# Neighbouring heads paired, w1 in one transfer, and a new opening order in a fused attention and expert kernel

## The chip, the cores and the metric

The kernel runs on one core of a Trainium2 chip. The metric is the device time of one execution in microseconds (us). Two executions of the same kernel differ by one or two per cent here, so kernels are compared by the runs of the same rounds on the same chip. Each run is marked fast or slow (slow: more than 1.5% above the fastest of its kernel), and verdicts use fast runs alone, with a 95% interval.

## The reference, cut to what matters

Two stages in one launch. First attention with short windows: 8 batches, 8 heads, 576 positions, 64 values per head. Heads 0 to 3 ("plain") see the last 32 positions, heads 4 to 7 ("dilated") every fourth of the last 128. Then a mixture of experts that picks one expert per batch.

```python
scores = (q @ k.transpose(0, 1, 3, 2)) / sqrt(64)        # [8, 8, 576, 576]
mask_plain = (rel >= 0) & (rel < 32)                     # heads 0..3
mask_dil   = (rel >= 0) & (rel < 128) & (rel % 4 == 0)   # heads 4..7
attn_out = softmax(where(mask, scores, -1e9)) @ v
x = attn_out.transpose(0, 2, 1, 3).reshape(8, 576, 512)  # head h is columns 64h..64h+63
logits = x.mean(axis=1) @ w_gate                         # [8, 8]
e = argmax(logits)                                       # one expert per batch
out = softmax(logits)[e] * (relu(x @ w1[e]) @ w2[e])     # w1: 512 x 1024, w2: 1024 x 512
```

## The kernel before: the parts that matter

A tile holds 128 partitions. Plain q and k are loaded with one transfer per batch: partition p holds 18 consecutive rows of the four heads laid end to end, so heads 0 and 1 lie in the lower 64 partitions and heads 2 and 3 in the upper 64. The loads turn float32 into bf16 on the way and are issued by GpSimd.

```python
def load_1(b, g, nm):                      # g == 0: plain heads, g == 1: dilated heads; RJ = 18
    nc.gpsimd.dma_start(
        out=loads[b][nm, g][:],
        in_=src[nm][b, 4 * g : 4 * g + 4].rearrange("h s d -> (h s) d").rearrange("(p j) d -> p j d", j=RJ))
```

TensorE turns each half of the tile with 64 x 64 transposes, so that a slot of attention works on one head of the lower half and one of the upper half at once: heads 0 and 2, then 1 and 3. Four slots make a batch, the dilated ones first. The rows of `w1` must follow the order of the heads in x, so each half of each chunk of 128 rows comes from another place and `w1` takes four transfers:

```python
for a in range(2):
    for g in range(2):
        r0 = 256 * g + 128 * a
        nc.gpsimd.dma_start(
            out=w1b[half(a), 2 * g : 2 * g + 2, f0 : f0 + fs],
            in_=moe_w1[ds(e_val, 1), r0 : r0 + 128, f0 : f0 + fs].rearrange("e (h d) f -> d (e h) f", d=DH))
load_vb(b + 2)          # GpSimd goes on issuing, in this order, for later batches
load_w2(e_val, w2b)
load_qa(b + 3); load_va(b + 3); load_qb(b + 3)
```

The expert is known only after the attention of its batch, so `w1` and `w2` cannot be loaded earlier. GpSimd issues everything in program order, loads that are needed two batches later and weights that are needed at once. In the steady part TensorE interleaves ffn1 (x times w1) and ffn2 (times w2) of batch b with the attention of batch b + 1.

The softmax here doesn't subtract the row's maximum and nothing guards it: scores larger than these inputs give would overflow.

Of the kernel before, what the change touches and what calls it, by code (L numbers as in the profile page):

```python
# [15 lines left out]
AF = mybir.ActivationFunctionType  # L16
# [3 lines left out]
P = 128  # L20
# [3 lines left out]
DH = 64  # L24
# [20 lines left out]
def kernel(  # L45
# [50 lines left out]
        return pools["M"].tile([P, 512 if dt == F32 else 1024], dt, name="m", tag="M", space=PSUM)[:]  # L96


    src = {"q": q, "k": k}
    loads = {}  # L100

# [8 lines left out]
        loads[b] = t  # L110

    def load_1(b, g, nm):
        nc.gpsimd.dma_start(
            out=loads[b][nm, g][:],
            in_=src[nm][b, 4 * g : 4 * g + 4].rearrange("h s d -> (h s) d").rearrange("(p j) d -> p j d", j=RJ),
        )

    def load_qk(b, g):
        for nm in ("k", "q"):
            load_1(b, g, nm)  # L120
# [24 lines left out]
    def load_va(b):  # L145
        if b < B:
            load_v(b, GO[0])
            load_vt(b, GO[0])
# [17 lines left out]
    dtt = const.tile([P, 4, 16], I32, name="dtt")  # L166
    for a in range(2):
        nc.gpsimd.iota(dtt[:, 2 * a : 2 * a + 2, :], pattern=[[1, 2], [2, 16]], base=32, channel_multiplier=-1)
    load_qk(0, GO[1])
    load_va(0)  # L170
    load_vb(0)
    load_qa(1)
    load_va(1)
# [7 lines left out]
    ones1 = const.tile([1, P], F32, name="ones1")  # L181
    nc.vector.memset(ones1[:], 1.0)
    wg_t = const.tile([P, 4, E], F32, name="wg_t")
    for a in range(2):
        for g in range(2):
            r0 = 256 * g + 128 * a
            nc.sync.dma_start(
                out=wg_t[64 * a : 64 * a + 64, 2 * g : 2 * g + 2, :],
                in_=moe_w_gate[r0 : r0 + 128, :].rearrange("(h d) e -> d h e", d=DH),
            )  # L190

    ident2 = const.tile([P, DH], BF16, name="ident2")
    nc.vector.tensor_tensor(out=ident2[:], in0=identb[:, 0:DH], in1=identb[:, DH:P], op=ALU.add)
# [51 lines left out]
    def emit_T(b, g, nm, banks=None):  # L245
        s = state(b)
        if g not in s["qk"]:
            s["qk"][g] = qkp.tile([P, 2, 2 * S], BF16, name="qk", tag="qk")
        qk = s["qk"][g][:, 0 if nm == "k" else 1, :]
        ld = loads[b][nm, g]  # L250
        tps = [early_bank(x, k, BF16) if banks else bank(BF16) for x, k in banks or ((0, 0), (0, 0))]
        ev = []
        if g == 0:
            for jh in range(2):
                tp = tps[jh][:, 0 : RH * DH].rearrange("p (j d) -> p j d", d=DH)
                for j in range(RH):
                    for u in range(2):
                        nc.tensor.transpose(  # L258
                            out=tp[half(u), j, :], in_=ld[half(u), RH * jh + j, :], identity=ident2[half(u), :]
                        )  # L260
                o = qk.rearrange("p (n j) -> p n j", j=RJ)[:, :, RH * jh : RH * jh + RH]
                i = tp.rearrange("p j n -> p n j")
                ev.append((o, i))
        else:
            for jh, (j0, j1) in enumerate(((0, 5), (5, 9))):
                tp = tps[jh][:, 0 : (j1 - j0) * P].rearrange("p (j n) -> p j n", n=P)
                for j in range(j0, j1):
                    nc.tensor.transpose(  # L268
                        out=tp[:, j - j0, :], in_=ld[:, 2 * j : 2 * j + 2, :].rearrange("p j d -> p (j d)"), identity=identb[:]
                    )  # L270
                o = qk.rearrange("p (n j) -> p n j", j=RH)[:, :, j0:j1]
                i = tp.rearrange("p j n -> p n j")
                ev.append((o, i))

        def on_dve():
            nc.vector.tensor_copy(out=ev[0][0], in_=ev[0][1])  # L276

        def on_act():
            nc.scalar.activation(out=ev[1][0], in_=ev[1][1], func=AF.Copy)  # L279

        return on_dve, on_act


    def emit_S_mm(b, n):
        s = state(b)
        g, h2 = GO[n // 2], n % 2
        qk = s["qk"][g]
        ps = ps0
        s["ps"] = ps

        def mm(a, e, o, lhsT, rhs):
            nc.tensor.matmul(  # L292
                ps[half(e), a, o : o + rhs.free_size()], lhsT=lhsT, rhs=rhs, start=True, stop=True, skip_group_check=True
            )

        if g == 0:
            kT = [qk[half(a), 0, S * h2 : S * h2 + S] for a in range(2)]
            qT = [qk[half(a), 1, S * h2 : S * h2 + S] for a in range(2)]
            for i in range(4):
                for e in range(2):  # L300
                    for a in range(2):
                        p0 = 128 * i + 64 * e
                        mm(a, e, QB * i, kT[a][:, p0 : p0 + KB], qT[a][:, p0 : p0 + QB])
            for a in range(2):
                mm(a, 0, 4 * QB, kT[a][:, 512:S], qT[a][:, 512:S])
            return

        u1 = (QB, 144)
        for i in range(4):
            o = HALF * (2 * (i // 2) + h2)  # L310
            for e in range(2):
                for a in range(2):
                    kc, qc = (qk[half(a), x, o : o + HALF].rearrange("p (m c) -> p c m", c=2)[:, i % 2, :] for x in range(2))
                    mm(a, e, QB * i, kc[:, 64 * e : 64 * e + KB], qc[:, 64 * e : u1[e]])
        for hh in range(2):
            o = HALF * (2 * hh + h2)
            for a in range(2):
                qc = qk[half(a), 1, o : o + HALF].rearrange("p (m c) -> p c m", c=2)
                mm(a, 0, 4 * QB + 32 * hh, qk[half(a), 0, o + 224 : o + HALF], qc[:, :, 128:144])
# [17 lines left out]
    def av_work(b, n):  # L337
# [26 lines left out]
            lasts.append(x)  # L364

        def V(a, e, i):
            return vm[half(e), 2 * a + h2, i, :]

        def pc(a, e, lo, hi):
            return pt[half(e), a, 0 : 4 * QB].rearrange("p (i n) -> p i n", n=QB)[:, :, lo:hi]  # L370
# [12 lines left out]
        def part_a():  # L383
# [8 lines left out]
                        mm(a, o + w * i, w, V(a, e, i), r, i == 0)  # L392
            if g == 0:
                for a in range(2):
                    mm(a, NLO + 256, 64, vt[:, 2 * a + h2, :], pt[half(0), a, 4 * QB : NP], False)
            for e in range(2):
                for a in range(2):
                    one = ones64[half(e), :]
# [23 lines left out]
        def part_b():  # L422
# [10 lines left out]
            if g == 0:  # L433
                for e in range(2):
                    for a in range(2):
                        o = DSO if e == 0 else DLO + 64
                        mm(
                            a, o, 256, ones64[half(e), :], pc(a, e, 64, 96), False,
                            lambda x: x.rearrange("p (i n) -> p i n", n=64)[:, :, 0:32],
                        )  # L440
            else:
                for r in range(2):
                    for a in range(2):
                        mm(
                            a, NLO, 320, vt[:, 2 * a + h2, r, :], pt[half(0), r, 4 * QB + 32 * a : 4 * QB + 32 * a + 32], False,
                            lambda x, r=r: tcls(x, 80)[:, r, :, 64:80],
                        )
                for a in range(2):
                    mm(a, DLO, 320, ones64[half(0), :], clss(a, 0, 64, 96), False, lambda x: tcls(x, 80)[:, :, :, 0:32])
                for a in range(2):  # L450
                    tl = pt[half(0), :, 4 * QB + 32 * a : 4 * QB + 32 * a + 32].rearrange("p t (c m) -> p t c m", c=2)
                    mm(a, DLO, 320, ones64[half(0), :], tl, False, lambda x: tcls(x, 80)[:, :, :, 64:80])
# [59 lines left out]
    def emit_gate(b):  # L512
# [14 lines left out]
        s["w1"], s["w2"] = w1b, w2b  # L527
        fs = F // 2 if b == 0 else F
        for f0 in range(0, F, fs):
            for a in range(2):  # L530
                for g in range(2):
                    r0 = 256 * g + 128 * a
                    nc.gpsimd.dma_start(  # L533
                        out=w1b[half(a), 2 * g : 2 * g + 2, f0 : f0 + fs],
                        in_=moe_w1[ds(e_val, 1), r0 : r0 + 128, f0 : f0 + fs].rearrange("e (h d) f -> d (e h) f", d=DH),
                    )
        if b == 0:
            load_1(2, GO[0], "q")
            load_va(2)
# [153 lines left out]
    for x, nm in enumerate(("k", "q")):  # L693
        for f in emit_T(0, a, nm, ((x, 0), (x, 1))):
            f()
    sl[0].sx()
    dve, act = emit_T(0, z, "k", ((1, 2), (1, 0)))
    sl[0].mask()
    dve()
    act()  # L700
    sl[1].sx()
    sl[0].av_a()
    dve, act = emit_T(0, z, "q", ((1, 1), (1, 2)))
    sl[0].av_b()
    dve()
    act()
    sl[1].mask()
    masks_b(band)
    sl[0].ln()
    sl[0].rd()  # L710
    sl[1].av_a()
    sl[2].sx()
    sl[1].av_b()
    sl[0].norm()
    sl[2].mask()
    sl[3].sx()
    sl[1].ln()
    sl[1].rd()
    sl[2].av_a()
    sl[2].av_b()  # L720
    sl[1].norm()
# [5 lines left out]
    sl[2].norm()  # L727
    sl[3].ln()
    sl[3].rd()
    sl[3].norm()  # L730
    dve0, act0 = emit_T(1, a, "k", ((0, 0), (0, 1)))
    dve0()
    act0()
    dve1, act1 = emit_T(1, a, "q", ((0, 2), (0, 0)))
    dve1()
    act1()
    emit_gate(0)
    sl[4].sx()
    dve0, act0 = emit_T(1, z, "k", ((1, 0), (1, 1)))
    sl[4].mask()  # L740
    dve0()
    act0()
# [2 lines left out]
    sl[4].av_b()  # L745
    sl[4].ln()
    sl[4].rd()
    dve1, act1 = emit_T(1, z, "q", ((1, 2), (1, 0)))
    sl[5].mask()
    dve1()  # L750
    act1()
# [80 lines left out]
```

## Time and profile before

| | before |
|---|---|
| median of 4 runs | 228.27 us (224.55 to 229.86) |
| span of the profiled run | 226.4 us |
| TensorE busy | 197.5 us |
| DMA issues for `w1` | 36, of 610 ns each on GpSimd |
| DMA issues for plain q and k | 16, whole tiles |

The prediction below shows the busy shares, the stretches and the chain. Four more lines of that page matter later: the clock of TensorE in 40 slices (9 is full speed), GpSimd's DMA queue (packets, MB, share), the chain that ended last by engine, and the loads of k (count, size, median us from issue to landing).

```profile
PEclk9999999998899999999999999999999999999998
...
q0 software_dynamic: 43584, 31.20, 94.8%
...
PE 67%; ACT 10%; DVE 8%; DMA 6%; issue 5%; POOL 1%; POOLq 0%; SPq 0%
...
km<-in_k_dram POOLq DMA_DIRECT2D x16, 288.0 KB, 12.8
```

The line shows one half clock stretch in the middle (54.5 to 57.9 us). It hides another: the first clock record of this trace comes at 40.8 us, and the view prints full speed before it. The matmuls say otherwise. A 128 x 288 matmul of ffn1 takes 447 ns before 40.8 us and again in the stretch in the middle, and 286 ns elsewhere. So the opening runs at half clock too, until 42.5 us in the changed kernel, and the granted clock of 1.00 for the first 36 us, in the stretches of the prediction and of the result, is only a missing record. The queue that carries nearly all loads has 43584 packets.

### The profile page before, as it was taken

Reading aid. Unit: us, or ns where it says so; the run is one execution under the profiler, and the core shown is the slowest. Engines: PE = TensorE matmul, PEld = TensorE weight load, DVE = VectorE, ACT = ScalarE, POOL = GpSimd, SP = SyncE. Lnnn points to the kernel's source line nnn. Section 1 sums busy time; section 2 is a strip of 40 time slices with the busy share of each in tenths; the row PEclk is TensorE's granted clock in tenths of the full one; section 3 lists DMA queues with packets and bytes.
Section 4 is the critical chain, followed back from the end, with each engine's and each line's share of the span. In section 5 each row is a group of like instructions: output and inputs, shape, how many; then the busy total and the mean of one; then the engine's idle time right before and its main releaser. Section 6 shows DMA issues by size and latency. Waiting matters only on the chain.

```text
span 226.4 us, 8318 instructions
## 1 busy us (share of the span) xinstructions
PE 197.5 (87%) x3584; PEld 136.7 (60%) x3584; DVE 128.9 (57%) x365; ACT 129.6 (57%) x230; POOL 87.6 (39%) x142
## 2 busy tenths in 40 slices
PE   0764668976999999999999999889999999999992
PEld 0663556764657775677567765666577647746741
DVE  4455555765566666666666757665676567415312
ACT  2566475764764776676667665668647763431420
POOL 7884078613764065505660277008300500230000
PEclk9999999998899999999999999999999999999998
DMA  5999469999999999999999999999994499399823
GB/s 82 176 187 190 67 91 172 204 209 166 170 169 237 253 201 174 236 241 212 193 236 239 219 196 219 209 233 170 181 233 132 74 157 239 121 143 257 178 93 116
DMA packets 50084, 41.18 MB, mean 182 GB/s; under 512 B 23936, under 2 KB 38272, under 8 KB 50048
## 3 DMA queue, kind: packets, MB, share of 16 engines
q0 software_dynamic: 43584, 31.20, 94.8%
q1 hardware_dynamic: 6464, 9.46, 12.3%
q8 instruction: 28, 0.46, 0.8%
q14 instruction: 8, 0.07, 0.1%
HBM read 62.41 MB, written 9.44 MB: 317 GB/s over the span
## 4 chain that ended last, share of the span: by engine, by line
PE 67%; ACT 10%; DVE 8%; DMA 6%; issue 5%; POOL 1%; POOLq 0%; SPq 0%
PE m L585 22%; PE m L605 22%; PE nd L360 6%; ACT pt L325 5%; PE m L258 4%; ACT qk L279 4%; DVE pt L332 4%; DMA w1b<-in_moe_w_dram 3%; PE m L268 3%; DMA vm<-in_v_dram 3%; PE m L620 3%; PE ps L292 3%; DVE ht L592 2%; PE e L360 1%; DVE xt L494 1%
## 5 line engine op out<-in xcount | busy, mean ns | idle before, releaser
L585 PE MATMUL m<-xt,w1b 128*128 128x288 bf16 x512 | 70.8, 294 | 1.8 <-DVE ht L592 1.6
L585 PEld LDWEIGHTS <-w1b 128*128 128x128 bf16 x512 | 49.4, 100 | 17.4 <-issue 3.4
L605 PE MATMUL m<-w2b,ht 128*128 128x512 bf16 x256 | 57.7, 380 | 0.0
L533 POOL DMA_DIRECT2D w1b<-in_moe_w_dram x36 | 21.5, 610 | 84.2 <-PE m L585 62.9
L590 ACT ACTIVATE ht<-m 128x288 bf16<-128x288 f32 x64 | 26.3, 411 | 29.8 <-PE m L585 26.5
L605 PEld LDWEIGHTS <-ht 128*128 128x128 bf16 x256 | 23.9, 98 | 27.8
L332 DVE TENSOR_TENSOR pt<-pt,mk 128x896 bf16<-128x896 bf16 x32 | 20.0, 624 | 28.4 <-ACT pt L325 28.4
L592 DVE TENSOR_SCALAR ht<-m 128x288 bf16<-128x288 f32 x64 | 27.4, 451 | 8.9 <-PE m L585 8.2
L325 ACT ACTIVATE pt<-ps 128x896 bf16<-128x896 f32 x32 | 28.9, 904 | 5.4 <-PE ps L292 5.4
L494 DVE SCALAR_TENSOR_TENSOR xt<-nd,rd 128x320 bf16<-128x320 f32 (+1 forms) x54 | 27.1, 539 | 7.5 <-ACT rd L467 7.5
L279 ACT ACTIVATE qk<-m 128x512 bf16<-128x512 bf16 (+1 forms) x24 | 17.5, 731 | 16.5 <-PE m L258 13.4
L126 POOL DMA_DIRECT2D vm<-in_v_dram x32 | 24.2, 776 | 3.2 <-DMA qm<-in_q_dram 1.5
L360 PEld LDWEIGHTS <-vm 64*64 64x64 bf16 x896 | 15.6, 114 | 14.6 <-issue 5.6
L276 DVE COPY qk<-m 128x640 bf16<-128x640 bf16 (+1 forms) x24 | 18.9, 787 | 7.4 <-PE m L258 4.8
L360 PE MATMUL nd<-pt,vm 64*64 64x64 bf16 (+1 forms) x760 | 18.2, 194 | 5.3 <-issue 3.1
L467 ACT ACTIVATE rd<-lnd 128x576 f32<-128x576 f32 x32 | 21.8, 683 | 1.0
L612 DVE TENSOR_SCALAR osb<-m,gbc 128x512 f32<-128x512 f32 x16 | 12.0, 751 | 16.1 <-PE m L605 16.1
L461 ACT ACTIVATE lnd<-nd 128x576 f32<-128x576 f32 x27 | 17.4, 644 | 5.3 <-PE nd L360 5.3
L292 PE MATMUL ps<-qk 64*64 64x96 bf16 (+3 forms) x608 | 15.7, 213 | 3.0 <-ACT qk L279 1.4
L292 PEld LDWEIGHTS <-qk 64*64 64x64 bf16 x608 | 15.5, 118 | 3.5 <-issue 3.3
L360 PE MATMUL nd<-pt,ones 64*64 64x256 bf16 (+2 forms) x244 | 16.3, 243 | 0.0
L610 ACT ACTIVATE osb<-m,gbc 128x512 f32<-128x512 f32 x16 | 10.9, 681 | 6.9 <-PE m L605 6.8
(72 smaller groups left out, 199.6 us busy)
## 6 DMA issues: line engine op xcount, KB each, us to landing
w2b<-in_moe_w_dram POOLq DMA_DIRECT2D x8, 1024.0 KB, 13.9
out_dram<-osb SPq DMA_DIRECT2D x32, 256.0 KB, 6.4
w1b<-in_moe_w_dram POOLq DMA_DIRECT2D x28, 256.0 KB, 6.4
km<-in_k_dram POOLq DMA_DIRECT2D x16, 288.0 KB, 12.8
qm<-in_q_dram POOLq DMA_DIRECT2D x16, 288.0 KB, 12.9
vm<-in_v_dram POOLq DMA_DIRECT2D x8, 256.0 KB, 10.3
vm<-in_v_dram POOLq DMA_DIRECT2D x32, 64.0 KB, 7.5
w1b<-in_moe_w_dram POOLq DMA_DIRECT2D x8, 128.0 KB, 5.6
```

Of the source, the lines that this page charges most:

```text
L126: nc.gpsimd.dma_start(out=t[:, h], in_=v[b, h, 0:512, :].rearrange("(c p) d -> p c d", p=P))
L279: nc.scalar.activation(out=ev[1][0], in_=ev[1][1], func=AF.Copy)
L292: nc.tensor.matmul(ps[half(e), a, o : o + rhs.free_size()], lhsT=lhsT, rhs=rhs, start=True, stop=True, skip_group_check=True)
L325: nc.scalar.activation(out=pt[:], in_=s["ps"][:, :, 0:NP], func=AF.Exp, scale=0.125)
L332: nc.vector.tensor_tensor(out=pt[:], in0=pt[:], in1=mk[:, g : g + 1, :].to_broadcast([P, 2, NP]), op=ALU.mult)
L360: x = nc.tensor.matmul(oo, lhsT=lhsT, rhs=rhs, start=start, stop=True, skip_group_check=True)
L467: nc.scalar.activation(out=rd[:], in_=s["lnd", n][:], func=AF.Exp, scale=-1.0)
L494: nc.vector.scalar_tensor_tensor(out=o, in0=a0, scalar=1.0, in1=a1, op0=ALU.mult, op1=ALU.mult, accum_out=s["pool"][:, w, c : c + 1],)
L585: nc.tensor.matmul(hm, lhsT=s["w1"][:, c, fc * P : (fc + 1) * P], rhs=s["xt"][:, c, cols], start=(c == 0), stop=(c == 3))
L590: nc.scalar.activation(out=o, in_=hm, func=AF.Relu)
L592: nc.vector.tensor_scalar_max(out=o, in0=hm, scalar1=0.0)
L605: nc.tensor.matmul(om, lhsT=s["ht"][:, fc, r * P : (r + 1) * P], rhs=s["w2"][:, fc, :], start=(fc == 0), stop=(fc == 7))
```

## The change

The intent: pair neighbouring heads (0 and 1, 2 and 3), so that x has w1's own row order and `w1` can come as one transfer. The dilated heads need only another index. The plain heads need their tile filled otherwise, the even heads in the lower half and the odd ones in the upper. That is two transfers of half a tile each. Also, V of the dilated heads is loaded ahead of plain q and k, and the opening (the first six slots) is ordered anew.

```diff
     def load_1(b, g, nm):
+        t = loads[b][nm, g]
+        h = src[nm][b, 4 * g : 4 * g + 4]
+        if g == 0:
+            for u in range(2):
+                nc.gpsimd.dma_start(
+                    out=t[64 * u : 64 * u + 64], in_=h.rearrange("(a u) (m j) d -> u a m (j d)", u=2, j=RJ)[u]
+                )
...
+    load_va(0)
     load_qk(0, GO[1])
-    load_va(0)
...
-            o = HALF * (2 * (i // 2) + h2)
+            o = HALF * (2 * h2 + i // 2)
...
-            for a in range(2):
-                for g in range(2):
-                    r0 = 256 * g + 128 * a
-                    nc.gpsimd.dma_start( ... a quarter of w1 ... )
+            nc.gpsimd.dma_start(
+                out=w1b[:, :, f0 : f0 + fs],
+                in_=moe_w1[ds(e_val, 1), :, f0 : f0 + fs].rearrange("e (c p) f -> p (e c) f", p=P),
+            )
...   (w_gate in one transfer; V indexed by 2 * h2 + a)
@@ the opening, cut: the q transposes of the plain heads now stand ahead of the first AV product,
   the mask of slot 2 ahead of the normalisation of slot 0, and the four evacuations of batch 1's dilated k and q on ScalarE
```

In the half loads, u names the half of the tile, a the head in it, m a run of 18 rows. As built, the source pattern is 2 x 32 x 1152 elements (a, m, run) and the destination 64 partitions x 1152.

## The prediction

> **What bounds the kernel now.** I read the summary page first (engine shares and the 40 slices), then the busy time by stretches, then the chain that ended last, then the single waits inside it. From the page:
>
> ```profile
> span 226.4 us, 8318 instructions
> PE 197.5 (87%) x3584; PEld 136.7 (60%) x3584; DVE 128.9 (57%) x365; ACT 129.6 (57%) x230; POOL 87.6 (39%) x142
> PE   0764668976999999999999999889999999999992
> DMA  5999469999999999999999999999994499399823
> q8 instruction: 28, 0.46, 0.8%
> ```
>
> TensorE is full from about the tenth slice (57 us) on. The first slices are not. The stretches give the sizes (busy us of each engine in each stretch, then granted clock, DMA share, GB/s):
>
> ```profile
> 0.00:10.00 10.00, 3.22 (x61) 2.82 (x63) 4.29 (x13) 3.04 (x4) 8.57 (x21) 1.00 0.78 122
> 10.00:20.00 10.00, 6.68 (x230) 5.60 (x224) 4.95 (x12) 7.66 (x14) 7.13 (x12) 1.00 1.50 194
> 20.00:28.00 8.00, 4.06 (x88) 3.33 (x91) 5.21 (x20) 3.69 (x7) 0.57 (x2) 1.00 0.93 102
> 28.00:36.00 8.00, 5.05 (x185) 4.74 (x177) 4.14 (x11) 5.04 (x10) 6.09 (x10) 1.00 0.71 101
> 60.00:136.00 76.00, 74.51 (x1432) 51.03 (x1431) 49.70 (x142) 50.23 (x92) 35.16 (x54) 1.00 1.25 214
> ```
>
> In the first 36 us (attention of batch 0 and the start of batch 1, no expert work yet) TensorE works 3.22 + 6.68 + 4.06 + 5.05 = 19.0 us and idles 17. From 60 to 136 us it idles 1.5 of 76. So a change that leaves TensorE's work alone gains in the first 36 us, or nearly nowhere. The chain that ended last says what the opening hangs on (start, length, what):
>
> ```profile
> 4.98 7.05 DMA vm<-in_v_dram
> 12.08 0.69 PE e L360 x14
> ...
> 24.46 0.85 DVE xt L494 x4
> 25.50 0.74 DVE qk L276
> 26.29 0.60 PE e L268 x4
> 26.91 0.74 ACT qk L279
> 27.69 0.50 PE ps L292 x13
> ...
> 46.08 1.00 issue
> ...
> 51.35 1.99 issue
> ```
>
> Three things are to be seen. V of the dilated heads lands at 12.03, and the first AV product starts at once. The dilated scores of batch 1 (27.69) hang on evacuations of the transposes of q and k that stand on VectorE behind the last normalisation of batch 0. And TensorE twice stops for 1 to 2 us for nothing that the profile shows.
>
> **What the Trainium skill says.** (1) "DMA: Bandwidth & Descriptors", section "Rules for kernel authors", on two transfers to disjoint partition halves: they serialize, as both use all 16 engines; use one transfer. The trace agrees: the four w1 quarters issued at 177.28 us land 4.4 us (first) to 7.2 us (last, issued 1.77 later) after their issues, so a quarter every (179.05 + 7.2 - 177.28 - 4.4) / 3 = 1.5 us. One transfer saves issue time, not data time. (2) Same page, "Why a DMA increments its semaphore by 16 and not by 1": the number of engines is the largest up to 16 that divides the slowest dimension of both access patterns, with an exception for some GpSimd copies that spread over partitions. All loads of the kernel before have 64 or 128 there; no run yet shows a smaller one. (3) "Runtime: NRT & Kernel Launch", "Instruction fetch mechanics": instructions come in blocks of 16 KiB, 256 each, by DMA. The trace agrees: 28 packets and 0.46 MB are 16 KB each, and TensorE's 3584 matmuls and 3584 weight loads are 7168 = 28 x 256. The unexplained stops at 46.08 and 51.35 are 256 TensorE instructions apart, as are two more at 141.72 and 148.51 (1.1 and 0.9 us), so I read all four, 5.0 us in sum, as late instruction blocks. The page calls this mostly hidden; this trace does not.
>
> **The change, part by part.**
>
> *Pairing of heads.* Chunk c of x now holds heads 2c and 2c+1, the order of w1's rows. Matmuls, exponentials, masks and evacuations stay the same in number and shape, so TensorE's 197.5 us stay. Cost: 0.
>
> *w1 in one transfer.* 36 issues become 9 (two for batch 0). An old issue takes 610 ns: 21.5 us. A new one names 128 x 4 rows, as each V issue of 776 ns does, so about 9 x 0.78 = 7.0 us. GpSimd saves about 14.5 us, but it is 39% busy. On the path this counts in two places. After the first gate, 8 issues (5.0 us, 29.29 to 34.30) become 2 (1.6 us); the first ffn1 at 37.4 waits for four of the old eight, landed by 36.6, so this keeps w1 ahead of an earlier TensorE, worth 0 by itself. After the last gate the quarters land at 205.9 against matmuls ready at 205.5: an idle 0.18 us. Gain 0.2.
>
> *k and q of the plain heads in halves.* 16 issues become 32, at 0.55 us: 9 us more on GpSimd, hidden. But the built program gives these halves a source pattern of 2 x 32 x 1152 and a destination of 64 x 1152. The slowest source dimension is 2.
>
> *Order of loads and engines in the opening.* Old landings in the trace: k and q dilated 5.6 and 7.1, k and q plain 9.1 and 10.7, V dilated 12.0 and 12.4. The stream runs at about 190 GB/s, a 288 KB load each 1.5 us. New order: V dilated at 8.5 and 8.9, k plain about 10.5, q plain about 12. The same five loads end at about 12, so the first slot gains little. I walked the new order by hand with durations of the trace: transposes 1.1 to 1.2 us, evacuations 0.73 to 0.83, exponential 0.92, mask 0.63, the two logarithms 0.70, reciprocal 0.68, normalisation 1.2 or 1.0, scores 0.6, AV about 1.2 with its fence.
>
> - k transposes end at 11.6, second scores 12.1, q transposes (q at 12.0) 13.3, first AV 13.3 to 14.4. Old: 12.08 to 14.1.
> - third scores 14.4 (old 15.1); fourth 16.0 (old 16.8); mask of slot 3 ends 19.7 (old 21.4), because it no longer stands behind two reciprocals and two normalisations; AV of slot 3 ends 20.9 (old 22.9); its reciprocal 22.3 (old 24.4).
> - the four evacuations of batch 1's dilated k and q are all on ScalarE, 4 x 0.74 from 22.3 to 25.3, while VectorE normalises; the gate's matmuls start at 23.4 (old 26.8).
> - scores of slot 4 at 25.3 (old 27.69).
>
> From there to the first AV in the late pool (34.67) the code is the same but for bank numbers, so that point moves by -2.4 us, and with it all that follows.
>
> Sum: -2.4 - 0.2 = -2.6 us.
>
> **Rivals.** *A: all moves as above.* The three times of before are 224.55, 228.84 and 229.86, the profiled run was 228.07; I start from 228.3, so 225.7. For it: the new order puts the q transposes ahead of the first AV, which makes sense only if q lands about when AV is ready.
>
> *B: the halved loads run on 2 of 16 engines.* One engine moves 190 / 16 = 12 GB/s, so 147 KB on two engines take 74 KB / 12 = 6.1 us, not 0.8. The four halves may run side by side on eight engines, behind the earlier loads, from about 8.7: k and q land near 15. Estimated walk: k transposes 16, scores 16.6, q transposes 17.8, first AV after that, third scores at about 18 in place of 14.4: +3.6. That makes 225.7 + 3.6 = 229.3. For it: the pattern in the built program and the skill's rule; against it: its exception for GpSimd, and the chosen order. I give it 0.35. In later batches these loads have over 20 us to spare.
>
> *C: the instruction blocks decide.* In the steady part a block comes when DMA queues are full. If larger w1 transfers delay them, TensorE stops more often; if the traffic falls elsewhere, some of the 5 us of stops go. Either sign, size up to about 2 us; the 5 us between the three times of before suggest such scatter. It widens the range and shifts nothing.
>
> *D: the gain is given back.* DMA share is 1.25 from 60 to 136 us, so loads could become the limit when TensorE comes earlier. Against it: TensorE waits for w1 only 0.2 us in the whole run, and fewer, larger w1 transfers leave room for later loads to be issued sooner. At most 1 us.
>
> **Range and chances.** 0.65 x 225.7 + 0.35 x 229.3 = 227.0; the middle of the distribution lies nearer A, so I say 226.3. C and the scatter give about 2 us to either side of each branch: 222.8 to 230.0. Two per cent are 4.6 us: faster by that needs A and lucky instruction blocks, 0.17; slower by that needs B and unlucky ones, 0.07; within 2%, 0.76.
>
> **What would show it.** In the new profile: plain k and q landing at about 10.5 and 12 (A) or near 15 (B); the gate's matmuls at about 23.5 and slot 4's scores at about 25.3; the first late-pool AV at about 32.3; busy time of TensorE from 60 us on unchanged; the sum of unexplained stops near 5 us. I would be wrong if the opening kept its 34.7 us with w1 and loads in place (then the hand-made walk missed a wait, of ScalarE above all, which gets two more evacuations), if the opening is won and the steady part loses it, or if the stops vanish or double.

## The result

The changed kernel takes 243.97 us in the median of 4 runs (242.86 to 245.72), all fast. Ratios in this document are the mean time of one kernel's fast runs over that of the other's fast runs of the same rounds, so they are not quite the ratio of the medians. Here the ratio is 1.0796 (1.0610 to 1.0982): slower by 8%. The predicted range ended at 230.0.

The page of the changed kernel, the same lines as before:

```profile
span 243.4 us, 8230 instructions
...
PE 202.5 (83%) x3584; PEld 139.2 (57%) x3584; DVE 127.8 (53%) x363; ACT 130.5 (54%) x232; POOL 85.5 (35%) x131
...
PE   0348668769991699979999999699999999999992
...
PEclk9999999958997589999999999979999999999999
...
q0 software_dynamic: 57744, 31.26, 92.3%
...
PE 43%; DMA 40%; POOL 5%; ACT 4%; issue 3%; DVE 3%; POOLq 1%
...
w1b<-in_moe_w_dram POOLq DMA_DIRECT2D x7, 1024.0 KB, 12.1
...
km<-in_k_dram POOLq DMA_DIRECT2D x16, 144.0 KB, 10.9
```

Read it against before: DMA makes 40% of the chain that ended last, where it made 6%. TensorE has a hole in the thirteenth slice (73 to 79 us), deep in the part that was full. Its busy time grew by 5.0 us although it does the same matmuls, and the clock line shows why: after the opening there are three stretches at half clock (the trace gives 49.3 to 56.2, 76.6 to 86.9 and 158.6 to 162.0 us, 20.4 us in sum, against 3.4 us before). TensorE was busy 14.9 us in them, against 3.4; at 447 ns for 286 that makes about 4.1 us of the 5.0, an estimate. The Trainium skill, "TensorE: Matmul & The Clock Gate", Part 1, says that the clock halves after an idle window of about 3.4 us. The trace agrees in the unit, for the stretches here are 6.8, 10.2 and 3.4 us long, and each comes with a wait of TensorE for a load; but only the second of these waits (7.0 us) is longer than 3.4, the others are 1.9 and 2.6. And the queue moved the same 31 MB in 14,160 more packets.

The stretches of the changed kernel (busy us of each engine with instructions, clock, DMA share, GB/s). The last one is a single microsecond in which hardly anything but the half loads of batch 0 moved (47 packets of theirs and 8 of V; four loads of V were under way too, and made almost no headway):

```profile
10.00:20.00 10.00, 4.14 (x140) 3.52 (x143) 2.58 (x4) 3.27 (x5) 4.85 (x9) 1.00 1.02 125
...
28.00:36.00 8.00, 5.30 (x164) 4.66 (x161) 3.83 (x13) 6.11 (x11) 5.28 (x9) 1.00 0.98 118
60.00:136.00 76.00, 66.29 (x1215) 44.82 (x1215) 44.31 (x125) 42.86 (x77) 32.33 (x47) 0.93 1.16 183
...
13.40:14.40 1.00, 0.00 (x0) 0.00 (x0) 0.00 (x0) 0.00 (x0) 0.00 (x0) 1.00 0.58 109
```

From 60 to 136 us TensorE idles 9.7 us, where it idled 1.5. And in the single microsecond every engine stands still while the four half loads move 109 GB/s at a share of 0.58, where the kernel before moved 194 on average from 10 to 20 us. Four loads on two engines each are eight of sixteen, a share of about one half. The share alone is no proof, as such shares go up to 1.50 here; the counts under "Four engines in place of two" say more. The chain (start, length, what) tells where the time went:

```profile
7.26 10.31 DMA qm<-in_q_dram
...
44.66 15.04 DMA qm<-in_q_dram
...
62.61 18.42 DMA w1b<-in_moe_w_dram
81.03 0.05 issue
81.08 6.91 PE m L584 x32
...
143.59 15.01 DMA w1b<-in_moe_w_dram
158.60 0.05 issue
158.65 5.70 PE m L584 x32
```

A half load of q takes 10.31 us to land in the opening, w1 of batch 1 takes 18.42, and then 32 ffn1 matmuls take 6.91 us at half clock (4.03 at full clock, at 108.93 of the same trace). The table gives starts read from the traces; the last two columns belong to experiments below (half loads with another source order, in all batches, second run, and in batch 0 alone). AV is the product of the attention weights and V; the late pool is the set of accumulator banks used after the opening, so its first AV marks the end of the opening.

| start of, us | before | changed | spread, all batches | spread, batch 0 only |
|---|---|---|---|---|
| gate of batch 0 | 26.80 | 29.40 | 24.29 | 23.96 |
| first AV in the late pool | 34.67 | 37.59 | 32.49 | 32.16 |
| ffn2 of batch 0 | 59.50 | 63.00 | 56.14 | 58.76 |
| ffn1 of batch 1 | 70.67 | 81.08 | 67.16 | 73.69 |
| ffn1 of batch 2 | 94.31 | 108.86 | 91.78 | 101.17 |
| ffn1 of batch 4 | 143.06 | 158.65 | 139.97 | 150.34 |
| end | 226.43 | 243.38 | 223.29 | 235.76 |

The changed kernel is 2.9 us behind at the end of the opening and 14.6 behind at ffn1 of batch 2. The larger part is lost where the prediction saw room.

### The profile page after: what moved, and what is told of

It is laid out like the page before. It is cut to its first block, busy times and chain, and to the rows that moved or that the text cites. A ratio compares the mean times of both kernels' runs of the same rounds, so it can differ in the third digit from the quotient of the medians.

```text
span 243.4 us, 8230 instructions
## 1 busy us (share of the span) xinstructions
PE 202.5 (83%) x3584; PEld 139.2 (57%) x3584; DVE 127.8 (53%) x363; ACT 130.5 (54%) x232; POOL 85.5 (35%) x131
## 3 DMA queue, kind: packets, MB, share of 16 engines
q0 software_dynamic: 57744, 31.26, 92.3%
## 4 chain that ended last, share of the span: by engine, by line
PE 43%; DMA 40%; POOL 5%; ACT 4%; issue 3%; DVE 3%; POOLq 1%
PE m L584 17%; PE m L604 15%; DMA w1b<-in_moe_w_dram 14%; DMA qm<-in_q_dram 10%; DMA w2b<-in_moe_w_dram 7%; DMA vm<-in_v_dram 4%; DMA km<-in_k_dram 4%; PE nd L362 3%; PE m L260 2%; PE m L619 2%; ACT pt L327 2%; ACT qk L281 2%; DVE pt L334 2%; PE m L270 1%; DVE ht L591 1%
## 5 line engine op out<-in xcount | busy, mean ns | idle before, releaser
L584 PE MATMUL m<-xt,w1b 128*128 128x288 bf16 x512 | 74.2, 305 | 11.2 <-DMA w1b<-in_moe_w_dram 9.7
L584 PEld LDWEIGHTS <-w1b 128*128 128x128 bf16 x512 | 51.6, 104 | 28.8 <-DMA w1b<-in_moe_w_dram 9.9
L532 POOL DMA_DIRECT2D w1b<-in_moe_w_dram x9 | 7.1, 785 | 45.5 <-PE m L584 21.9
L362 PEld LDWEIGHTS <-vm 64*64 64x64 bf16 x896 | 16.4, 115 | 9.4 <-issue 2.9
L362 PE MATMUL nd<-pt,ones 64*64 64x256 bf16 (+2 forms) x244 | 17.0, 247 | 1.5 <-issue 1.5
L118 POOL DMA_DIRECT2D qm<-in_q_dram x16 | 10.6, 671 | 21.7 <-DMA w2b<-in_moe_w_dram 11.2
L294 PE MATMUL ps<-qk 64*64 64x96 bf16 (+3 forms) x608 | 16.3, 215 | 1.9 <-ACT qk L281 1.7
## 6 DMA issues: line engine op xcount, KB each, us to landing
w1b<-in_moe_w_dram POOLq DMA_DIRECT2D x7, 1024.0 KB, 12.1
km<-in_k_dram POOLq DMA_DIRECT2D x16, 144.0 KB, 10.9
qm<-in_q_dram POOLq DMA_DIRECT2D x16, 144.0 KB, 10.2
```

What stands on the lines that cost most here:

```text
L294: nc.tensor.matmul(ps[half(e), a, o : o + rhs.free_size()], lhsT=lhsT, rhs=rhs, start=True, stop=True, skip_group_check=True)
L362: x = nc.tensor.matmul(oo, lhsT=lhsT, rhs=rhs, start=start, stop=True, skip_group_check=True)
L584: nc.tensor.matmul(hm, lhsT=s["w1"][:, c, fc * P : (fc + 1) * P], rhs=s["xt"][:, c, cols], start=(c == 0), stop=(c == 3))
```

## The experiments

The theory: the half loads run on 2 of the 16 DMA engines each, because the slowest dimension of their source is 2. So they land late in the opening and, in later batches, linger and hold up w1, w2 and the rest. Rivals: the one large w1 transfer lands later than four quarters; the new order of the engines is bad; two transfers for one are bad in themselves, whatever their pattern.

### The same half loads with 32 as the slowest dimension

The two source dimensions change places, so partition 2m + a of a half holds what 32a + m held. The transposes put it right with a permuted identity, as many as before. The result passes the check, and the index arithmetic gives the same transposed tile.

```diff
-in_=h.rearrange("(a u) (m j) d -> u a m (j d)", u=2, j=RJ)[u]
+in_=h.rearrange("(a u) (m j) d -> u m a (j d)", u=2, j=RJ)[u]
-identity=ident2[half(u), :]
+identity=ident2[half(u), :].rearrange("p (m a) -> p a m", a=2)
```

> The changed kernel with one thing altered: each half-load of plain k and q takes its source rows in the order 32 x 2 (row block, then head) in place of 2 x 32, and the transposes read the identity in a permuted order to undo it. Same number of transfers, same bytes, same partition halves. Theory E (the 2 x 32 source puts each half-load on 2 of 16 engines): plain k lands near 10.5 us and plain q near 12, the 4-byte packets fall from 16272 to about 2000, no wait for w1 over 1 us is left, and the time is 225 to 228 us. Theory W (one large w1 transfer is what starves TensorE): unchanged, 242 to 245. Theory O (the new engine orders lose the opening): the first late-pool AV stays at 37 us or later although k and q are early.

Measured: 225.93 us, ratio 0.9926 (0.983 to 1.0021). Its profile fell in a slow run, so I ran it once more in another call:

> x1 once more beside x5 and x9 on the same chip. If one w1 transfer costs something where the loads are spread, it is 1 us or more above x5; if the two are equal within 0.5 us, the form of w1's transfer is worth nothing here, against 6.5 us where the loads run on two engines.

Measured: 225.47 us, ratio 0.9975 (0.9917 to 1.0033), all fast. Its page:

```profile
span 223.3 us, 8216 instructions
...
q0 software_dynamic: 43408, 31.20, 95.1%
...
w1b<-in_moe_w_dram POOLq DMA_DIRECT2D x7, 1024.0 KB, 8.9
...
km<-in_k_dram POOLq DMA_DIRECT2D x16, 144.0 KB, 11.4
```

One exchange of two dimensions takes back all 18 us. The order of the engines stays as in the changed kernel and so does the single w1, so neither costs anything like this by itself. The packets fall from 57744 to 43408. Beware of the last line: the median landing of k is no shorter than in the changed kernel (10.9), presumably because most of these loads stand in a long queue anyhow. A median over all batches hides what matters; w1's landing (12.1 there, 8.9 here) does not.

### w1 in four again

```diff
-nc.gpsimd.dma_start(out=w1b[:, :, f0 : f0 + fs], in_=... "e (c p) f -> p (e c) f")
+for a in range(2):
+    for g in range(2):
+        nc.gpsimd.dma_start(out=w1b[half(a), 2*g : 2*g+2, f0 : f0+fs],
+            in_=moe_w1[ds(e_val, 1), 256*g : 256*g+256, f0 : f0+fs].rearrange("e (c p) f -> p (e c) f", p=P)[half(a)])
```

> The changed kernel with w1 in four transfers again (plain k and q still in 2 x 32 halves). Theory W: the wait for w1 of batch 1 goes and the time comes back to about 230. Theory E: no gain, 241 to 247, the opening the same as in the changed kernel (plain q landing near 17.5).

Measured: 250.49 us, ratio 1.0938 (1.082 to 1.1057). Two of its five runs are slow; the mean of its fast runs is 249.2 us, against 244.1 for the changed kernel in another call, 5 us less. The fast runs don't overlap, the intervals of the ratios do, so the size is uncertain. The single w1 is not the cause; it seems to soften the loss. Then the same beside spread half loads, in two calls:

> The spread version (x1) with w1 in four transfers again. If w1 in one transfer is worth its issue time alone, as the prediction had it, the time rises by 0 to 1 us over x1's 225.9. If the number of transfers under way at once matters (as x2 against the changed kernel, 250.5 to 244.0, suggests), it rises by 3 us or more.

> x5 once more, to see whether its lead over x1 (224.5 to 225.9) holds beside other runs of the kernel before: 224 to 225 if it does, 225.5 to 226.5 if it was scatter.

Measured: 224.54 us, ratio 0.9858 (0.9814 to 0.9902), and 224.39 us, ratio 0.9925 (0.9873 to 0.9977). Against 225.93 and 225.47 with one transfer, four quarters are about 1 us better or equal. So the worth of one w1 transfer depends on the loads beside it: about 5 us where they are narrow, nothing or less where they are spread. I would explain this by the number of transfers under way (below): four quarters take four places, one takes one. No run varies that alone.

### The pattern alone, in the kernel before

If the pattern is the cause, it must cost the old kernel too, and two halves with a wide pattern must not. Both runs split plain q and k of the kernel before in two halves, nothing else changed. The first uses the narrow source and so puts heads 0 and 2, 1 and 3 where 0 and 1, 2 and 3 belong: wrong on purpose. (It still passed the tolerance, presumably since the attention weights are nearly equal within a window. A pass proves little here.)

```diff
+# first run:  source 2 x 32, wrong heads
+in_=h.rearrange("(a u) (m j) d -> u a m (j d)", u=2, j=RJ)[u]
+# second run: source 64, right heads
+in_=h.rearrange("(u a) (m j) d -> u (a m) (j d)", u=2, j=RJ)[u]
```

> The kernel before with one thing altered: plain k and q as two half-loads each with a 2 x 32 source (heads 0 and 2, then 1 and 3; the result is wrong on purpose, the work is the same). Theory E: most of the loss appears here without any other part of the change, 238 to 246 us, about 16000 packets of 4 bytes. Theories W and O: about 228.

> The kernel before with plain k and q as two half-loads each, source 64 rows in their natural order (result right). Control for the splitting itself: theory E expects 227 to 230, plain k and q landing within 1 us of before; if issuing more transfers is what costs (GpSimd's time, or its limit of transfers under way), it is 235 or more.

Measured: 252.66 us, ratio 1.109 (1.0989 to 1.1192), and 228.33 us, ratio 1.0045 (0.995 to 1.014). The queue lines of their pages, first the narrow one:

```profile
q0 software_dynamic: 58176, 31.26, 93.5%
```

```profile
q0 software_dynamic: 43840, 31.20, 94.5%
```

Two halves cost nothing that these runs resolve; two narrow halves cost 24 us, with the old w1 and the old order.

### Four engines in place of two

If the number of engines is what counts, a source of 4 x 16 must give about half the stretch. This takes heads 0 to 3 in each half and is again wrong on purpose.

```diff
-in_=h.rearrange("(a u) (m j) d -> u a m (j d)", u=2, j=RJ)[u]
+in_=h.rearrange("a (u m j) d -> u a m (j d)", u=2, j=RJ)[u]
```

> The changed kernel with a 4 x 16 source in place of 2 x 32 for the halves of plain k and q (rows of the wrong heads on purpose; same bytes, same transfers). By the skill's rule each half then runs on 4 engines, so four halves fill all 16: each engine has 16 rows, 3.1 us. Idle engines matter (theory E in its plain form): plain k and q land by about 13, the time is 225 to 229, near x1. The 4-byte packets matter by themselves (14 idle engines x 32 of them in each half-load, now 12 x 16, so about 8100 in all): some 40% of the loss stays, 232 or more.

Measured: 229.61 us, ratio 1.0086 (1.002 to 1.0152), with this queue line:

```profile
q0 software_dynamic: 49552, 31.23, 98.0%
```

Plain k of batch 0 landed at 12.66 and 13.02 us and q at 14.0 and 14.29. The changed kernel has 15.07, 15.55, 15.76 and 17.58; the second spread run has 9.7, 10.77, 11.73 and 12.48. So the landings lie between, but most of the time is back already: the loss is far from linear in the number of engines.

The packets give the number of engines in two ways. A row of these loads is a packet of 2304 bytes, and the number of them under way at once, in the median over a stretch in which they dominate, is 9 in the changed kernel (13.4 to 14.4 us), 15 here (10.5 to 12.5) and 16 with spread halves (9.7 to 11.7): eight busy engines against about sixteen. And packets of 4 bytes on this queue, counted in the traces, are 1936 with spread halves (16 for each of the 121 transfers), 8080 here, 16272 in the changed kernel. There are 32 half loads. (16272 - 1936) / 32 = 448 = 14 x 32, and (8080 - 1936) / 32 = 192 = 12 x 16: this fits if each idle engine gets as many tiny packets as a busy one has rows. With 2 x 32, 2 engines carry 32 rows each and 14 idle; with 4 x 16, 4 engines carry 16 rows each and 12 idle. How much of the 3.7 us between this run and the spread one (of another call) is the tiny packets and how much the later landings stays open.

### Where the loss is made: spread halves in batch 0 alone

The two edits of the first experiment, only `if b == 0`. If the opening made the loss, nearly all would be back.

> The changed kernel with the half-loads spread (32 x 2 source) for batch 0 alone; the other seven batches keep the 2 x 32 source. The prediction's claim was that later batches have 20 us to spare, so only the opening suffers: then this repairs nearly all, 226 to 230. If the loss is made in the later batches, through transfers that linger while only eight may be under way, the first late-pool AV comes back to about 33 and the time is still 238 or more.

Measured: 238.61 us, ratio 1.0488 (1.0352 to 1.0624). Taking the changed kernel's 243.97 from its own call, 5.4 us are back and 10.9 stay (238.61 against 227.72 for the kernel before in this call; the means of the fast runs give 6.2 and 11.1). Two lines of its chain, then its largest wait of TensorE for w1 (us in total, times, longest):

```profile
57.94 15.70 DMA w1b<-in_moe_w_dram
...
73.69 6.42 PE m L585 x30
```

```profile
PE m L585 <- DMA w1b<-in_moe_w_dram: 7.1, 4, 3.5
```

Its opening is the fast one (first late AV at 32.16 us), and still w1 of batch 1 takes 15.70 us to land and TensorE waits for w1 7.1 us in sum. So two thirds of the loss (10.9 of 16.3) are made in later batches, whose half loads of k are issued 12 to 25 us before TensorE turns to them in the changed kernel. (The reverse run, with batch 0 alone narrow, was not made.) One of them is itself too late: k of batch 2, issued at 35.23 and 35.91 us, lands at 49.34 and 50.73, and TensorE waits 1.9 and 1.1 us for it; in this run it waits 3.8 us there.

How that comes about can be read in GpSimd's issues of the changed kernel (start, length, what, and in brackets the idle time before it and what ended that):

```profile
59.99 1.36 POOL L118 DMA_DIRECT2D km<-in_k_dram  x2 [0.79 <-DMA qm<-in_q_dram]
61.33 1.32 POOL L118 DMA_DIRECT2D qm<-in_q_dram  x2
62.61 0.85 POOL L532 DMA_DIRECT2D w1b<-in_moe_w_dram  x1
...
81.58 0.53 POOL L122 DMA_DIRECT2D qm<-in_q_dram  x1 [6.46 <-DMA w1b<-in_moe_w_dram]
```

The four half loads stand directly ahead of w1(1), and GpSimd itself had to wait for an older q before it could issue them. In all traces GpSimd issues no transfer before the eighth earlier one has landed: eight are under way at most. The limit is one of the built program and not shown to be one of the chip: the trace has the issues use eight semaphores in turn (99 to 106), and each waits for its own. A half load that lingers for 10 us or more keeps one of the eight places, and w1, w2 and the loads of later batches come later. The rate of transfer in the 19 us after 62 us, in 40 slices, shows the other half of it:

```profile
GB/s 79 64 48 51 63 73 91 89 87 109 183 161 153 195 191 166 200 194 72 144 218 232 279 299 290 256 209 209 206 211 194 202 236 261 276 298 271 282 242 239
```

For ten slices (4.75 us) the 16 engines move about 75 GB/s between them, just after 1 MB of w1 was asked for. That w1's shares on the engines of the half loads stood behind them is how I read this; the trace does not name the engine of a packet. The packet sizes support it: w1's first packet (2048 bytes) starts at 65.09 us, and from 65.4 to 68.4 us eight or nine of w1's packets are under way most of the time beside eight or nine of the half loads. Plain V of batch 0, issued behind the first half loads, shows the same: of its 2048 packets exactly half start by 14.4 us, and the other half only after it, when the half loads are nearly done. Why there are only four to seven rows of the half loads under way, and nothing of w1, for 2.5 us after w1's issue (62.61 us) stays open. So does how the loss divides between places and engines, since no run varies the limit of eight.

### The opening

Is the new order worth anything once the loads are spread? First the first experiment with the old order of loads and engines:

```diff
-load_va(0); load_qk(0, GO[1]); load_vb(0)
+load_qk(0, GO[1]); load_va(0); load_vb(0)      # and the old block of the first six slots
```

> The spread version with the load order and the engine orders of the kernel before: pairing, one w1 transfer and halves stay. If x1's gain in the opening is the new orders' (prediction: 2.4 us), the first late-pool AV goes back to 34.7 and the time to 227.5 to 228.5. If the gain came from w1's transfer, it stays near 226.

Measured: 227.03 us, ratio 0.9957 (0.9897 to 1.0017); the first late AV at 34.67, as before. Against 225.93 in the call before, on the same chip, the new order is worth about 1 us, less than the intervals. Then an order of my own: k of the plain heads transposed a step later, masks earlier, and q of batch 1 transposed ahead of k and shared between VectorE and ScalarE.

```diff
+sl[0].sx(); masks_b(band); sl[0].mask(); sl[1].sx(); sl[0].av_a()
+T(0, plain, k); sl[1].mask(); evacuate; sl[0].av_b(); T(0, plain, q); sl[0].ln(); evacuate; sl[0].rd() ...
+T(1, dilated, q) evacuated by VectorE and ScalarE; T(1, dilated, k) by ScalarE and VectorE; gate
```

> The spread version with an opening of my own: both dilated slots of batch 0 are scored before plain k and q arrive, the first AV goes before the plain transposes, and two of the four evacuations of batch 1's dilated q and k go to VectorE. By hand: slot 4's scores at 24.4 (x1: 25.98), first late-pool AV at 31.4 (x1: 32.96), so 1.5 us under x1, about 224.4. If the instruction blocks or the last w2 transfer give it back, the time equals x1's.

> My opening (x8) together with w1 in four transfers (x5), loads spread. If both small gains add: about 223.5 us, 1.5 to 2% under the kernel before. If x5's lead over x1 was scatter, it equals x8, 225 to 226.

Measured: 226.0 us, ratio 0.9911 (0.986 to 0.9962), and with w1 in four 225.35 us, ratio 0.9932 (0.9873 to 0.9991). The first late AV came at 31.53 us, earlier than any other, and the end did not follow. An opening that is 1 us shorter is no longer seen at the end. The version that beats both kernels in two calls is the changed one with spread half loads and w1 in four: below before by 1.4% and 0.75%, so about 1%.

## Why the prediction was wrong

**The step that failed** stands in rival B: "In later batches these loads have over 20 us to spare." It was not so even in the kernel before, whose plain k of batch 2 is issued at 37.04 us and first used at 44.94, 7.9 us later, and whose later batches have over 20 us from issue to use only from batch 4 on. In the changed kernel TensorE waits 3.0 us for k of batch 2. And the step left out what slow loads do to others, which is the larger part: the wait for w1 is 9.7 us. With narrow loads in the batches after the first alone, the kernel is 10.9 us above the kernel before and 12.7 above the spread one (238.61 - 225.93), and B had zero for them. B's whole size, 3.6 us against A, should have been 18.0 (243.97 - 225.93): 5.4 of it from batch 0 (243.97 - 238.61) and 12.7 from the others. The rest of the error is weight: B got 0.35, though the built program named the pattern and the skill the rule, and the exception it was set against did not apply.

**B's opening** was nearly right. Landings "near 15": measured 15.07 to 17.58. Scores predicted at 16.6: measured 16.38. q transposes "17.8": they start at 17.62. Third scores "about 18": measured 19.71, as the first AV stood behind the q transposes. +3.6 against A became +5.1 at the first late AV (37.59 against 32.49). So the opening's term was too small by 1.5 us, far less than the later batches' term.

**A, all moves as above**, is what the spread runs show: 225.9 and 225.5 us against the predicted 225.7. The second match is partly luck, for in that call the kernel before took 225.88 and not 228.3. The chain of the second spread run goes through the predicted steps:

```profile
6.84 5.63 DMA qm<-in_q_dram
12.52 1.01 PE e L260 x16
...
25.50 0.50 PE ps L295 x13
...
32.49 0.70 PE nd L363 x19
```

q landed at 12.5 (predicted 12), slot 4's scores start at 25.50 (25.3) and the first late AV at 32.49 (32.3). The gate came at 24.29 (23.4). One reason in the walk was wrong: the mask of slot 3 still stands behind two normalisations on VectorE. It ends at 20.00 (predicted 19.7, before 21.45) because the second of these starts at 18.25 in place of 19.70. The gain of the opening was 2.2 us in this trace and 1.7 in the other, for 2.4 predicted. At the end the ratios 0.9926 and 0.9975 are worth 1.7 and 0.6 us of about 228, for 2.6 predicted, so part of it is given back.

**w1 in one transfer**, "gain 0.2": with spread loads it is about -1 us (-1.4 and -1.1, hardly more than the noise), with narrow ones about +5. Nobody had asked what it is worth beside narrow loads.

**C, instruction blocks**: the unexplained stops were 5.0 us in sum before and 2.1 in the changed kernel's chain (1.54 at 107.15 and 0.57 at 114.48). That is 2.9 us less, where up to about 2 to either side were supposed, and it points away from the result: stops don't explain the loss.

**D, the gain is given back**, "at most 1 us" because "fewer, larger w1 transfers leave room for later loads": the wait for w1, 0.2 us before, became 9.7 us in two waits, 7.0 of them at 81.08 (us in total, times, longest; first before, then changed):

```profile
PE m L585 <- DMA w1b<-in_moe_w_dram: 0.2, 1, 0.2
PE m L584 <- DMA w1b<-in_moe_w_dram: 9.7, 2, 7.0
```

The mechanism of D, loads as the limit of the steady part, is what happened; its size was worked out for branch A alone. B and D were treated as rivals and were one chain of causes. What the prediction had asked to see was the right test: "busy time of TensorE from 60 us on unchanged" failed at once, with 66.29 us of 76 for 74.51.

## What to carry to other kernels

Before a transfer is split or reordered, look at the built access pattern on both sides: a slowest dimension of 32 or more did no harm here, 4 cost a few us and 2 cost 18. Two dimensions of one load can change places for nothing that these runs resolve, if a later transpose takes a permuted identity. A slow prefetch is not free because its own consumer is far away: check that distance batch by batch, and ask what shares its engines and its issuing queue, above all weights that are known late. And when two rivals are each judged small, ask what they do together.

## What the Trainium skill lacked or had wrong

- "DMA: Bandwidth & Descriptors", section "Why a DMA increments its semaphore by 16 and not by 1", gives the rule of the slowest dimension and an exception for some GpSimd copies. For a converting GpSimd load of 2 x 32 rows onto 64 partitions the rule held and the exception did not: 109 GB/s and 9 packets under way in the median while four such loads moved nearly alone (2 engines each), and 4 engines for 4 x 16 by the count of packets. The page does not say which GpSimd copies are excepted.
- The same section says that for a GpSimd load all 16 engines post a completion, whatever its shape. The trace agrees, with 16 packets of 4 bytes for each of 121 transfers where the loads are spread. It does not say that idle engines get more than that: 448 further packets per load with 2 engines, 192 with 4, so that 14336 of the changed kernel's 57744 packets on the queue were such.
- The same page, section "Rules for kernel authors", row "Use all 16 engines", warns of an outermost dimension below 16. It says nothing of what such a load costs others: 10.9 us of 16.3 here came from later batches; with batch 0 repaired TensorE waits 7.1 us for w1 and 4.2 us for such loads.
- The same section, row "Two transfers to disjoint partition halves", advises one transfer. Two wide halves for one cost nothing that the runs resolve (ratio 1.0045), and w1 in four instead of one was equal or 1 us better (224.5 and 224.4 against 225.9 and 225.5 us).
- "Runtime: NRT & Kernel Launch", section "Instruction fetch mechanics", calls the cost of a block boundary mostly hidden. The kernel before stops four times for 0.9 to 2.0 us, 5.0 us in sum, in two pairs 252 recorded TensorE instructions apart; each stop ends 2.3 to 2.4 us after a 16 KB packet starts on the instruction queue. That these are late blocks is read from this and was not tested.
- "TensorE: Matmul & The Clock Gate", Part 1, names an idle window of about 3.4 us in its table of the two states. The half clock stretches were multiples of that (6.8, 10.2 and 3.4 us), but two of the three came with a wait of only 1.9 and 2.6 us. It holds the ramp at the start below 1% of a typical span; here matmuls ran at half clock (447 ns for 286) until 40.8 us of 226.4. What that costs at the end no run isolates.
